# Forgetting attention and a GELU MLP on one core: batch 1's attention with its masks on TensorE and its side work reordered

## The chip, the cores and the metric

The kernel runs on one NeuronCore of a Trainium2 chip. The core has a matrix engine (TensorE, "PE" in the profile), a vector engine (VectorE, DVE), an activation engine (ScalarE, ACT), a general engine (GpSimd, POOL) and a queue engine (SyncE, SP) that starts transfers. The engines run side by side and wait for one another through semaphores. The metric is the device time of one execution in microseconds; lower is better.

## The reference, cut to what matters

Attention with a decay, over 8 batches of 8 heads, 576 tokens and 64 columns a head, then a two-layer MLP on the 4608 tokens:

```python
# q, k, v: (8, 8, 576, 64); f: (8, 8, 576); w_in: (512, 2048); w_out: (2048, 512)
scores = q @ k.T / sqrt(64)
cum    = cumsum(log(clip(f, 1e-4, 1)), axis=-1)
scores = where(causal, -1e9, scores + cum[..., :, None] - cum[..., None, :])
attn   = softmax(scores)
x      = (attn @ v), heads side by side          # (4608, 512)
h      = x @ w_in
out    = (0.5 * h * (1 + erf(h / sqrt(2)))) @ w_out
```

The kernel doesn't add the decay to the scores. The row's term cancels in the softmax, and the column's term becomes a weight exp(-cum) on the rows of v and on a column of ones beside them ("weighing"), whose product with the exponentials gives the softmax's sum. The causal mask only touches the five diagonal 128 x 128 blocks of a head; tokens 448 to 511 lie in two blocks and are weighted zero in one of them.

## The kernel before: the parts that the change touches

The program is one Python function whose order of calls is each engine's order of instructions. For each batch it does attention, head pair by head pair (HP = 4), with the second GEMM of the batch before as filling; then the first GEMM with GELU (`gemm1`). Batches 0 and 1 have attentions of their own. Pools give buffers in turn: two for scores (`s_psum`), two each of `o_psum` and `m_psum`, two for the tokens of q and of k (`qk_pool`), one for the weighed v (`v_pool`) and one for v itself.

One score tile: up to two products of kT and qT, the exponential, and the mask. `on_pe` chooses how the mask is made: on TensorE, as two more small products per diagonal block and head that add a large negative number to the future before the exponential, or on GpSimd, which sets the future to zero after it.

```python
def scores(b, i, t):
    on_pe = b == 0 or (b == 1 and i == 0)
    st = s_psum.tile([P, 2, 512], FP32, tag="s", name=f"s{t}")
    c = 0
    for n, q0, w in STILES[t]:
        masked = on_pe and c in SDIAG[t]
        for half in range(-1, 2 if masked else 0):
            for h in range(2):
                d = slice(h * D, (h + 1) * D)
                if half < 0:
                    to = st[:, h, c : c + w]
                    ab = kT[i][d, K0[n] : K0[n] + P], qT[i][d, q0 : q0 + w]
                else:
                    last = (half + 1) * D
                    to = st[:, h, c : c + last]
                    ab = key_of[d, half, :], after[d, half, 0:last]
                nc.tensor.matmul(to, *ab, start=half < 0, stop=half == 1 or not masked)
        c += w
    et = e_pool.tile([P, 2, 512], BF16, tag=f"e{t}", name=f"e{t}")
    nc.scalar.activation(et[:, :, 0:c], st[:, :, 0:c], Act.Exp, scale=scale)
    for c0 in [] if on_pe else SDIAG[t]:
        nc.gpsimd.affine_select(out=et[:, :, c0 : c0 + P], ...)   # cut
```

SDIAG has five entries over the four tiles of a head pair, so five masks a pair. The other pieces:

- `transposes_first(b, i, which, pool, tag)`: 12 TensorE transposes of the tokens of q (which 0) or k (1) of pair i into one buffer of the pool named, and a VectorE copy to qT or kT. Batches 0 and 1 are transposed so.
- `transpose_dma(b, h0, h1)`: the same by DMA for batches 2 and later, into `tq` and `tk`; `untangle(b, i)`: eight VectorE copies from there to qT and kT.
- `weigh_v(b, i)`: on GpSimd, the weighed v of a pair and its column of sums (two instructions). It needs v of the batch in place.
- `load_qk_tokens(b)`: GpSimd starts the loads of q and k of a batch. `load_v(b)`: SyncE starts five loads of v.
- `attend(b, i, h, ...)`: 15 products of exponentials and weighed v of one head ("AV"); `normalize`: a reciprocal and a multiplication on VectorE; `to_xT`: five TensorE transposes of a pair's result and a copy.

Batch 1's attention:

```python
FILL_1 = [[0, 0, 0, 0], [0, 0, 0, 0], [0, 0, 2, 2], [2, 2, 0, 0], [4]]

def second_attention():
    b, fill = 1, gemm2_half(0, 0)           # 16 products of batch 0's second GEMM

    def av(i, h):
        attend(b, i, h, (0, 1, 2, 3, 4))
        normalize(b, i, h)

    for i in range(HP):
        for t in range(4):
            scores(b, i, t)
            if (i, t) in ((0, 1), (0, 3)):
                for which in range(2):
                    transposes_first(b, 2 + t // 2, which, o_psum, "o")
            take(fill, FILL_1[i][t])
            if i and t == 1:
                av(i - 1, 0)
                av(i - 1, 1)
            if i and t == 3:
                to_xT(b, i - 1, nc.vector.tensor_copy, o_psum, "o")
            if (i, t) in ((1, 2), (2, 0)):
                weigh_v(1, i + 1)
            if (i, t) == (3, 0):
                load_qk_tokens(3)
                transpose_dma(2, 0, 4)
                transpose_dma(2, 4, 8)
    av(HP - 1, 0)
    take(fill, FILL_1[HP][0])
    av(HP - 1, 1)
    both = s_psum.tile([P, 2, 1024], BF16, tag="s", name="ps_x2")
    take(fill, 99)
    gemm1_begin(1, both)
    x_tail(1)
    load_v(2)
```

And the first GEMM's loop with what is threaded through it:

```python
for ffb in range(0 if b > 1 else 4, n_ff):      # n_ff = 16
    gemm1(b, ffb)
    if b == 0:
        if ffb in (13, 15):
            for which in range(2):
                transposes_first(1, ffb // 2 - 6, which, o_psum, "o")
        if ffb == 12:
            weigh_v(1, 0); load_w_out(0); load_w_out(1); weigh_v(1, 1)
            load_qk_tokens(2); load_w_out(2); load_w_out(3)
    elif b + 1 < B:
        first, gap = (5, 3) if b == 1 else (0, 4)
        at, late = divmod(ffb - first, gap)
        if late == 0:
            untangle(b + 1, at)
        if late == gap - 2:
            weigh_v(b + 1, at)
        if ffb == 14 and b > 1:
            load_qk_tokens(b + 2)
```

Although `load_qk_tokens(3)` is written ahead of `transpose_dma(2, ...)`, the built program makes GpSimd's loads of batch 3 wait for the semaphores of those DMA transposes.

Of the kernel before, what the change touches and what calls it, by code (L numbers as in the profile page):

```python
# [10 lines left out]
Act = mybir.ActivationFunctionType  # L11
# [7 lines left out]
HP = 4  # L19
# [31 lines left out]
def kernel(  # L51
# [10 lines left out]
    nc = tc.nc  # L62
# [24 lines left out]
    o_psum = ctx.enter_context(tc.tile_pool(name="o_psum", bufs=2, space=PSUM))  # L87
    m_psum = ctx.enter_context(tc.tile_pool(name="m_psum", bufs=2, space=PSUM))
# [4 lines left out]
    def load_qk_tokens(b, h0=0, h1=H):  # L93

        if b >= B:
            return
        if b not in qk_of:
            qk_of[b] = [
                qk_pool.tile([PT, H, JT * D], BF16, tag=n, name=f"{n}{b}")
                for n in "qk"  # L100
            ]
        for src, dst in zip((q, k), qk_of[b]):
            nc.gpsimd.dma_start(  # L103
                dst[:, h0:h1, :],
                src[b, h0:h1].rearrange("h (p j) d -> p h (j d)", j=JT),
            )
# [67 lines left out]
    warm = consts.tile([P, TC], BF16)  # L174
# [18 lines left out]
    def transposes_first(b, i, which, pool, tag):  # L193

        src = qk_of[b][which]
        ps = pool.tile([P, JT, PT], BF16, tag=tag, name="ps_f")
        for h in range(2):
            for j in range(JT):
                nc.tensor.transpose(
                    ps[h * D : (h + 1) * D, j, :],  # L200
                    src[:, 2 * i + h, j * D : (j + 1) * D],
                    ident_bf[:PT, :PT],
                )

        op = nc.scalar.copy if b == i == which == 0 else nc.vector.tensor_copy
        op(
            (qT, kT)[which][i].rearrange("d (p j) -> d p j", j=JT),
            ps.rearrange("d j p -> d p j"),
        )
# [3 lines left out]
    def transpose_dma(b, h0, h1):  # L213

        if b >= B:
            return
        if b not in tq_of:
            tq_of[b] = [
                tq_pool.tile([P, H, JT // 2, PT], BF16, tag="t" + n, name=f"t{n}{b}")
                for n in "qk"  # L220
            ]
        for src, dst in zip(qk_of[b], tq_of[b]):
            nc.sync.dma_start_transpose(  # L223
                dst[:, h0:h1].rearrange("d h j p -> d (h j) p"),
                src[:, h0:h1].rearrange("p h c -> p (h c)"),
            )
# [19 lines left out]
    def weigh_v(b, i, eng=nc.gpsimd):  # L246

        if b not in vw_of:
            vw_of[b] = v_pool.tile([P, H, NBLK, D + 1], BF16, tag="vw", name=f"vw{b}")
        hs = slice(2 * i, 2 * i + 2)  # L250
        bh = b * H + 2 * i
        w = wT[:, :, bh : bh + 2].rearrange("p n h -> p h n")
        eng.tensor_tensor(  # L253
            vw_of[b][:, hs, :, 0:D],
            v_sb[:, hs, :, :],
            w.unsqueeze(3).to_broadcast([P, 2, NBLK, D]),
            Alu.mult,
        )
        eng.tensor_copy(vw_of[b][:, hs, :, D], w)
# [1 line left out]
    e_of = {}  # L261

    def scores(b, i, t):
        on_pe = b == 0 or (b == 1 and i == 0)
        st = s_psum.tile([P, 2, 512], FP32, tag="s", name=f"s{t}")
        c = 0
        for n, q0, w in STILES[t]:
# [11 lines that stand above are left out]
                    nc.tensor.matmul(  # L279
                        to, *ab, start=half < 0, stop=half == 1 or not masked  # L280
                    )
            c += w
        et = e_pool.tile([P, 2, 512], BF16, tag=f"e{t}", name=f"e{t}")
        e_of[b, i, t] = et
        nc.scalar.activation(et[:, :, 0:c], st[:, :, 0:c], Act.Exp, scale=scale)  # L285
        for c0 in [] if on_pe else SDIAG[t]:
            nc.gpsimd.affine_select(  # L287
                out=et[:, :, c0 : c0 + P],
                in_=et[:, :, c0 : c0 + P],
                compare_op=Alu.is_ge,  # L290
                fill=0.0,
                base=0,
                pattern=[[0, 2], [1, P]],
                channel_multiplier=-1,
            )
# [3 lines left out]
    def attend(b, i, h, ms):  # L299
        if (b, i, h) not in o_of:  # L300
            o_of[b, i, h] = o_psum.tile([P, NBLK, D + 1], FP32, tag="o", name="o")
        o = o_of[b, i, h]
        for m in ms:
            for n in range(m + 1):
                t, c = where(n, m)
                nc.tensor.matmul(  # L306
                    o[:, m, :],
                    e_of[b, i, t][:, h, c : c + P],
                    vw_of[b][:, 2 * i + h, n, :],
                    start=(n == 0),  # L310
                    stop=(n == m),
                )
# [14 lines left out]
    def xT(b):  # L327
        if b not in xT_of:
            xT_of[b] = xT_pool.tile([P, n_dm, XC], BF16, tag="xT", name="xT")
        return xT_of[b]  # L330

    def to_xT(b, i, copy, pool=m_psum, tag="m", ps=None):
        if ps is None:
            ps = pool.tile([P, XC], BF16, tag=tag, name="ps_x")
        for m in range(NBLK):
            nc.tensor.transpose(
                ps[:, m * P : (m + 1) * P], x_of[b, i][:, m, :, :], ident_bf
            )
        copy(xT(b)[:, i, :], ps)  # L339
# [302 lines left out]
    def second_attention():  # L642


        b, fill = 1, gemm2_half(0, 0)

        def av(i, h):
            attend(b, i, h, (0, 1, 2, 3, 4))
            normalize(b, i, h)

        for i in range(HP):
            for t in range(4):
                scores(b, i, t)
                if (i, t) in ((0, 1), (0, 3)):
                    for which in range(2):
                        transposes_first(b, 2 + t // 2, which, o_psum, "o")
                take(fill, FILL_1[i][t])
                if i and t == 1:
                    av(i - 1, 0)
                    av(i - 1, 1)  # L660
                if i and t == 3:
                    to_xT(b, i - 1, nc.vector.tensor_copy, o_psum, "o")
                if (i, t) in ((1, 2), (2, 0)):
                    weigh_v(1, i + 1)
                if (i, t) == (3, 0):
                    load_qk_tokens(3)
                    transpose_dma(2, 0, 4)
                    transpose_dma(2, 4, 8)
        av(HP - 1, 0)
        take(fill, FILL_1[HP][0])  # L670
        av(HP - 1, 1)
# [6 lines that stand above are left out]
    for b in range(B):  # L678
        if b == 0:
            first_attention()  # L680
        elif b == 1:
            second_attention()
        else:
            attention(b)
        if b == 0:
            x_tail(0)
        for ffb in range(0 if b > 1 else 4, n_ff):
            gemm1(b, ffb)
            if b == 0:
                if ffb in (13, 15):  # L690
                    for which in range(2):
                        transposes_first(1, ffb // 2 - 6, which, o_psum, "o")
                if ffb == 12:
                    weigh_v(1, 0)
                    load_w_out(0)
                    load_w_out(1)
                    weigh_v(1, 1)
                    load_qk_tokens(2)
                    load_w_out(2)
                    load_w_out(3)  # L700
            elif b + 1 < B:
                first, gap = (5, 3) if b == 1 else (0, 4)
                at, late = divmod(ffb - first, gap)
                if late == 0:
# [5 lines that stand above are left out]
# [34 lines left out]
```

The softmax here doesn't subtract the row's maximum and nothing guards it: scores larger than these inputs give would overflow.

## Time and profile before

| | |
|---|---|
| device time, median of 3 (lowest to highest) | 363.75 us (363.01 to 365.11) |
| span of the profiled execution | 363.6 us |
| TensorE / ScalarE / VectorE / GpSimd busy | 94% / 59% / 53% / 35% |

The busy time of each engine by stretch of the profiled execution, read from its table of windows:

| stretch, us | what runs | TensorE | VectorE | ScalarE | GpSimd | TensorE clock |
|---|---|---|---|---|---|---|
| 0 to 24.5 | loads, attention 0 | 20.10 | 15.44 | 18.30 | 16.48 | 1.00 |
| 24.5 to 41.0 | first GEMM of batch 0 | 16.45 | 2.98 | 11.08 | 5.25 | 1.00 |
| 41.0 to 73.0 | attention 1 | 20.77 | 11.69 | 14.18 | 14.88 | 0.73 |
| 73.0 to 87.7 | first GEMM of batch 1 | 14.46 | 12.60 | 10.50 | 6.47 | 1.00 |
| 87.7 to 121.2 | attention 2, filled | 33.35 | 16.61 | 16.87 | 9.49 | 1.00 |
| 121.2 to 304.3 | batches 2 to 7 | 181.59 | 126.04 | 125.07 | 75.82 | 1.00 |
| 304.3 to 363.6 | last GEMMs | 55.69 | 7.38 | 19.10 | 0.40 | 0.99 |

How to read the profile's lines: "L287" is a line of the kernel; "out<-in" are the program's tiles; "x3" is the number of instructions merged into a line; a bracket at the end gives how long the engine had been idle before it and what ended that. In a timeline the first number is the start in us and the second the time that the line covers. A wait for several semaphores is put down to the one that came last by the profile. The clock is the share of full speed that TensorE was granted. The lines of this kernel that matter are: L279 score products and TensorE masks, L285 exponential, L287 GpSimd mask, L306 AV, L253 and L259 weighing, L103 token loads, L223 DMA transposes, L115 loads of v, L199 TensorE token transposes, L206 their copies, L237 untangling, L358 first GEMM, L484 and L449 second GEMM as filling.

### The profile page before, as it was taken

What the parts mean: (1) busy time and instruction counts of PE and PEld (TensorE: products, weight loads), DVE (VectorE), ACT (ScalarE), POOL (GpSimd) and SP (SyncE); (2) the same over time, 40 slices, a digit from 0 to 9 for tenths busy, and PEclk for the clock granted to TensorE, in tenths of its full rate; (3) what the DMA queues carried; (4) which work ended last, traced back from release to release, by engine and by line L of the source; (5) the groups of instructions that cost most, each with busy time, mean ns of one, the idle gap of its engine ahead of it and who ended that gap; (6) DMA issues with size and microseconds to landing.
All of it is one profiled execution on the core that took longest, in us unless ns stands there. A gap on an engine that the chain in (4) does not pass through costs nothing.

```text
span 363.6 us, 7947 instructions
## 1 busy us (share of the span) xinstructions
PE 342.4 (94%) x3232; PEld 179.9 (49%) x3232; DVE 192.7 (53%) x424; ACT 215.1 (59%) x295; POOL 128.8 (35%) x252
## 2 busy tenths in 40 slices
PE   7799886499999999999999999999999999999996
PEld 4574552244455445554555455545554555444443
DVE  5660442279346793579457955795579544011011
ACT  5977665077464378747874787478746874602610
POOL 8290762324332804452445344533451340000000
PEclk9999968599999999999999999999999999999999
DMA  8899999970978099919892899388920022011013
GB/s 126 153 176 192 192 196 191 184 120 2 196 144 162 29 138 211 160 59 130 166 199 69 124 149 205 87 120 160 203 80 2 32 65 77 0 57 60 0 31 87
DMA packets 99924, 43.03 MB, mean 118 GB/s; under 512 B 78704, under 2 KB 95344, under 8 KB 99888
## 3 DMA queue, kind: packets, MB, share of 16 engines
q1 hardware_dynamic: 82592, 28.37, 39.1%
q0 software_dynamic: 16896, 13.63, 25.1%
q8 instruction: 25, 0.41, 0.5%
q10 hardware_dynamic: 400, 0.52, 0.4%
q14 instruction: 11, 0.09, 0.1%
HBM read 36.85 MB, written 9.44 MB: 127 GB/s over the span
## 4 chain that ended last, share of the span: by engine, by line
PE 74%; DMA 10%; ACT 7%; POOL 5%; SPq 2%; issue 1%; DVE 0%; POOLq 0%; ACTq 0%; DVEq 0%
PE ps L358 30%; PE ps L449 20%; PE ps L391 8%; PE o L306 7%; PE s L279 5%; DMA k<-in_k_dram 5%; ACT e L285 4%; DMA v_sb<-in_v_dram 4%; PE ps L484 2%; ACT L285 2%; POOL vw L253 1%; DMA tq<-q 1%; POOL q L103 1%; SPq L223 1%; ACT g L375 1%
## 5 line engine op out<-in xcount | busy, mean ns | idle before, releaser
L375 ACT ACTIVATE g<-ps 128x512 bf16<-128x512 f32 x144 | 85.3, 597 | 79.3 <-PE ps L358 79.3
L285 ACT ACTIVATE e<-s 128x896 bf16<-128x896 f32 (+1 forms) x128 | 104.0, 863 | 35.2 <-PE s L279 34.2
L358 PE MATMUL ps<-xT,w_in_sb 128*128 128x512 bf16 x512 | 112.7, 379 | 0.2 <-ACT ot L493 0.2
L449 PE MATMUL ps<-w_out_sb,g 64*128 64x512 bf16 (+1 forms) x751 | 109.2, 376 | 0.0
L287 POOL TENSOR_SCALAR_AFFINE_SELECT e<-e 128x256 bf16<-128x256 bf16 x135 | 53.4, 406 | 111.3 <-ACT e L285 110.4
L358 PEld LDWEIGHTS <-w_in_sb 128*128 128x128 bf16 x576 | 56.0, 98 | 67.6 <-issue 2.3
L449 PEld LDWEIGHTS <-g 64*128 64x128 bf16 (+1 forms) x751 | 40.0, 94 | 30.8 <-issue 3.3
L237 DVE COPY qT<-tq 64x288 bf16<-64x288 bf16 x96 | 51.7, 539 | 1.4
L279 PE MATMUL s<-qT,kT 64*128 64x320 bf16 (+4 forms) x384 | 46.7, 285 | 5.5 <-ACT e L285 4.3
L306 PE MATMUL o<-vw,e 128*128 128x65 bf16 x960 | 42.4, 198 | 8.9 <-POOL e L287 8.6
L306 PEld LDWEIGHTS <-e 128*128 128x128 bf16 x960 | 37.4, 101 | 24.8 <-issue 10.0
L253 POOL TENSOR_TENSOR vw<-v_sb,wT 128x640 bf16<-128x640 f32 x31 | 39.7, 1281 | 15.6 <-DMA v_sb<-in_v_dram 11.2
L457 DVE COPY ot<-ps 128x512 f32<-128x512 f32 x26 | 17.9, 689 | 40.1 <-PE ps L449 40.1
L237 DVE COPY kT<-tk 64x288 bf16<-64x288 bf16 x96 | 33.8, 352 | 1.6
L279 PEld LDWEIGHTS <-kT 64*128 64x128 bf16 x384 | 20.2, 94 | 26.5 <-issue 14.2
L319 DVE RECIPROCAL r<-o 128x5 f32<-128x5 f32 x64 | 12.3, 192 | 39.0 <-PE o L306 38.5
L320 DVE TENSOR_TENSOR x<-o,r 128x320 bf16<-128x320 f32 x64 | 31.4, 491 | 2.4 <-DVE r L319 0.2
L400 DVE COPY ot<-ps 128x512 f32<-128x512 f32 (+2 forms) x9 | 5.7, 632 | 48.6 <-PE ps L391 48.6
L391 PE MATMUL ps<-w_out_sb,g 128*128 128x512 bf16 (+2 forms) x144 | 28.0, 355 | 0.0
L391 PEld LDWEIGHTS <-g 128*128 128x128 bf16 x144 | 13.5, 98 | 14.5
L459 DVE TENSOR_TENSOR ot<-ot,ps 128x512 f32<-128x512 f32 x26 | 17.9, 687 | 1.5
L348 POOL COPY tails<-xT 128x256 bf16<-128x256 bf16 x8 | 3.2, 399 | 34.4 <-DVE xT L339 34.4
(61 smaller groups left out, 162.1 us busy)
## 6 DMA issues: line engine op xcount, KB each, us to landing
out_dram<-ot SPq DMA_DIRECT2D x32, 256.0 KB, 2.2
v_sb<-in_v_dram SPq DMA_DIRECT2D x24, 256.0 KB, 4.6
q<-in_q_dram POOLq DMA_DIRECT2D x6, 576.0 KB, 6.0
k<-in_k_dram POOLq DMA_DIRECT2D x6, 576.0 KB, 8.6
v_sb<-in_v_dram SPq DMA_DIRECT2D x22, 128.0 KB, 5.8
w_in_sb<-in_moe_w_in_dram POOLq DMA_DIRECT2D x4, 512.0 KB, 7.4
w_out_sb<-in_moe_w_out_dram POOLq DMA_DIRECT2D x4, 512.0 KB, 12.0
q<-in_q_dram POOLq DMA_DIRECT2D x4, 144.0 KB, 4.0
```

Of the source, the lines that this page charges most:

```text
L237: nc.vector.tensor_copy(rows[:, odd], src[odd * D : (odd + 1) * D, 2 * i + h].rearrange("d j p -> d p j"),)
L253: eng.tensor_tensor(vw_of[b][:, hs, :, 0:D], v_sb[:, hs, :, :], w.unsqueeze(3).to_broadcast([P, 2, NBLK, D]), Alu.mult,)
L279: nc.tensor.matmul(to, *ab, start=half < 0, stop=half == 1 or not masked)
L285: nc.scalar.activation(et[:, :, 0:c], st[:, :, 0:c], Act.Exp, scale=scale)
L287: nc.gpsimd.affine_select(out=et[:, :, c0 : c0 + P], in_=et[:, :, c0 : c0 + P], compare_op=Alu.is_ge, fill=0.0, base=0, pattern=[[0, 2], [ ...
L306: nc.tensor.matmul(o[:, m, :], e_of[b, i, t][:, h, c : c + P], vw_of[b][:, 2 * i + h, n, :], start=(n == 0), stop=(n == m),)
L320: nc.vector.tensor_tensor(x_of[b, i][:, :, h, :], o[:, :, 0:D], r.unsqueeze(2).to_broadcast([P, NBLK, D]), Alu.mult,)
L358: nc.tensor.matmul(ps, w_in_sb[:, kt, ffb * P : (ffb + 1) * P], src[:, kt, 0:TC], start=(kt == 0), stop=(kt == n_dm - 1),)
L375: nc.scalar.activation(g_of[c][ffb], ps, Act.Gelu)
L391: nc.tensor.matmul(pss[ts][:, c0:c1], g_of[c][kt][:, ts * P : (ts + 1) * P], w_out_sb[:, kt, c0:c1], start=(kt == 0), stop=(kt == n_ff - 1),)
L449: nc.tensor.matmul(banks[r], g_of[c][kt][rows, ts * P : (ts + 1) * P], w_out_sb[rows, kt, :], start=(kt == 0), stop=last if r else kt == n ...
L457: nc.vector.tensor_copy(ot, banks[1])
```

## The change

Only batch 1 is changed, with what is threaded through the first GEMMs around it.

- All masks of batch 1 are made on TensorE, not only those of the first head pair. GpSimd has no mask left in that attention.
- The two heads' AV products, which stood together after tile 1 of the next pair, stand after tiles 1 and 2.
- The token transposes of pair 1 leave the first GEMM of batch 0; those of pairs 1, 2 and 3 follow the first three score tiles, in `o_psum`, `m_psum` and `o_psum`. Pair 0's come one block later than before (after block 14 instead of 13).
- `weigh_v` of pairs 2 and 3 is done ahead of the attention, as GpSimd's first work there.
- A 1 x 1 exponential ahead of the attention makes ScalarE load the exponential's table before the first scores are there.
- The transposes of a pair's result (`to_xT`) come one pair later, for the last two after the loop.
- `load_qk_tokens(3)` moves from the attention's last pair to block 4 of the first GEMM of batch 1, behind the attention and `x_tail`.

```diff
     def scores(b, i, t):
-        on_pe = b == 0 or (b == 1 and i == 0)
+        on_pe = b < 2
...
+        def transposes(i, pool, tag):
+            for which in range(2):
+                transposes_first(b, i, which, pool, tag)
+
+        nc.scalar.activation(warm[0:1, 0:1], warm[0:1, 0:1], Act.Exp)
+        weigh_v(1, 2)
+        weigh_v(1, 3)
         for i in range(HP):
             for t in range(4):
                 scores(b, i, t)
-                if (i, t) in ((0, 1), (0, 3)):
-                    for which in range(2):
-                        transposes_first(b, 2 + t // 2, which, o_psum, "o")
+                if i == 0 and t < 3:
+                    transposes(t + 1, *((m_psum, "m") if t == 1 else (o_psum, "o")))
                 take(fill, FILL_1[i][t])
-                if i and t == 1:
-                    av(i - 1, 0)
-                    av(i - 1, 1)
-                if i and t == 3:
-                    to_xT(b, i - 1, nc.vector.tensor_copy, o_psum, "o")
-                if (i, t) in ((1, 2), (2, 0)):
-                    weigh_v(1, i + 1)
+                if i and t in (1, 2):
+                    av(i - 1, t - 1)
+                if i > 1 and t == 0:
+                    to_xT(b, i - 2, nc.vector.tensor_copy, o_psum, "o")
                 if (i, t) == (3, 0):
-                    load_qk_tokens(3)
                     transpose_dma(2, 0, 4)
                     transpose_dma(2, 4, 8)
+        to_xT(b, HP - 2, nc.vector.tensor_copy, o_psum, "o")
         av(HP - 1, 0)
...
             if b == 0:
-                if ffb in (13, 15):
+                if ffb == 14:
                     for which in range(2):
-                        transposes_first(1, ffb // 2 - 6, which, o_psum, "o")
+                        transposes_first(1, 0, which, o_psum, "o")
...
             elif b + 1 < B:
+                if b == 1 and ffb == 4:
+                    load_qk_tokens(3)
                 first, gap = (5, 3) if b == 1 else (0, 4)
```

## The prediction

> **What bounds the kernel now.** I read the slices of the page first, then the chain of waits, then the timelines of single engines between 36 and 105 us, where the change lies. The page gives TensorE 94% busy, but its PE row has one hole and its PEclk row one dip, both between slices 5 and 8 (9.09 us each, so 45 to 73 us): batch 1's attention. Everything after 75 us is paced by TensorE without gaps, so a change in this stage is worth what it moves the start of that gapless part. The chain of waits there:
>
> ```profile
> 43.46 12.26 DMA k<-in_k_dram
> 55.73 3.97 SPq L223
> 59.76 4.79 DMA tq<-q
> ...
> 65.14 0.84 POOL q L103
> ...
> 66.62 0.77 POOL k L103
> 67.40 0.78 POOL e L287 x2
> ```
>
> From 43 to 68 us no arithmetic is on the chain. The tokens of batch 2 land, are transposed by DMA, only then may GpSimd issue the load of batch 3, and only then does it come to three masks of batch 1's last head pair. TensorE's own timeline shows the price:
>
> ```profile
> 60.43 0.22 PE L306 MATMUL o<-vw,e 128*128 128x65 bf16 x2
> 68.23 1.08 PE L306 MATMUL o<-vw,e 128*128 128x65 bf16 x13 [7.57 <-POOL e L287]
> 69.12 1.90 PE L484 MATMUL ps<-w_out_sb,g 128*128 128x512 bf16 x4
> ...
> 72.97 0.59 PE L358 MATMUL ps<-xT,w_in_sb 128*128 128x512 bf16 x2
> ...
> 87.66 0.37 PE L279 MATMUL s<-qT,kT 64*128 64x256 bf16 x4
> ```
>
> 7.57 us idle, then four projection matmuls in 1.90 us, about twice what eight take later. The first GEMM of batch 1 starts at 72.97 and attention 2 at 87.66, so that stage is 14.69 us. GpSimd over the same time:
>
> ```profile
> 57.94 0.77 POOL L287 TENSOR_SCALAR_AFFINE_SELECT e<-e 128x256 bf16<-128x256 bf16 x2 [0.92 <-ACT e L285]
> 65.14 0.84 POOL L103 DMA_DIRECT2D q<-in_q_dram  x1 [6.44 <-DMA tq<-q]
> 66.62 0.77 POOL L103 DMA_DIRECT2D k<-in_k_dram  x1 [0.64 <-DMA tk<-k]
> 67.40 1.12 POOL L287 TENSOR_SCALAR_AFFINE_SELECT e<-e 128x256 bf16<-128x256 bf16 x3
> ...
> 80.05 1.40 POOL L253 TENSOR_TENSOR vw<-v_sb,wT 128x640 bf16<-128x640 f32 x1 [4.37 <-PE ps L358]
> ```
>
> The last line is the one I come back to: weighing for batch 2 starts at 80.05. TensorE, which the view names, had long been done with batch 1's values; asking for batch 2's v load by its tile shows who it was. Its last transfer is issued at 67.9 and needs 12.0 us, which is 79.9:
>
> ```profile
> L115 SPq DMA_DIRECT2D v_sb<-in_v_dram x1: 5374/5374/5374, 67.9 to 67.9; - x1
> ...
> DMA to landing us min/median/max: 12.0/12.0/12.0
> ```
>
> Last, what a stage of this kind costs when masks are on TensorE: batch 0's attention, by ScalarE and TensorE.
>
> ```profile
> 14.94 7.40 ACT L285 ACTIVATE e<-s 128x640 bf16<-128x640 f32 x9 [0.56 <-PE s L279]
> ...
> 19.27 0.37 PE L279 MATMUL s<-qT,kT 64*128 64x320 bf16 x4
> 19.47 0.25 PE L279 MATMUL s<-after,key_of 64*128 64x64 bf16 x4
> 19.66 0.65 PE L306 MATMUL o<-vw,e 128*128 128x65 bf16 x15
> 20.24 0.36 PE L279 MATMUL s<-qT,kT 64*128 64x448 bf16 x2
> ```
>
> Nine exponentials in 7.40 us, 0.82 each; a masked score tile 0.39 (19.27 to 19.66), one head's AV product 0.58 (19.66 to 20.24).
>
> [...]three selects whose inputs were ready by about 61 us run at 67.40, behind two loads.[...]after the transposes at 41.8 to 45.0 with gaps of 1.03 and 0.36 us, the granted clock of this trace was 0.50 at 46 to 48 us; but batch 0, with transposes too, kept 1.00.[...]the rows of the table loads have a mean of 1283 ns.
>
> **The change part by part.** I date the new stage from rows of this trace, at full clock.
>
> 1. Start. One pair of token transposes (q and k of a head pair, 0.75 to 1.1 us) now lies ahead of the last gelu block instead of two. The scores begin about 40.3 instead of 41.0, when VectorE has copied kT. The gelu that ends at about 41.0 is followed by the table load without waiting for scores: 41.0 + 1.28 + about 0.15 for the 1x1 exponential (my estimate) puts the first real exponential at 42.4 instead of 42.93. Worth 0.5 us at most.
>
> 2. Masks. 15 selects of 0.39 us leave GpSimd; 15 mask groups of four matmuls join TensorE, about 0.09 to 0.14 us each by batch 0's starts, 1.8 us in all. They are real TensorE time, but the AV products no longer wait for GpSimd: its two waits of 1.00 and 7.57 us go.
>
> 3. Loads and weighing. The load of batch 3 now stands after the attention, so it blocks no mask. Two weighings of 1.46 us (1.27 + 0.19) move to the front: the second half of v lands at 36.9 + 6.6 = 43.5, GpSimd is free at 45.8, so both are done by 48.8, and the first AV product to need them comes at about 54.
>
> 4. TensorE's sum. Score tiles by batch 0's starts: 0.47, 0.39, 0.38, 0.32 = 1.56 us for a head pair. Pair 0: 1.56 + 3 transposes x 1.10 = 4.9. Pair 1: 1.56 + 2 AV x 0.58 = 2.7, but ScalarE needs 3 x 0.82 + 0.65 = 3.1, so 3.1. Pairs 2 and 3: 2.7 + 0.29 (x transposes, 21.52 to 21.81) + 4 fills x 0.216 = 3.9 each. Tail: 0.29 + 2 x 0.58 + 8 x 0.216 = 3.2, and about 0.5 waiting for the last exponential. Sum 4.9 + 3.1 + 3.9 + 3.9 + 3.7 = 19.5. From 40.3: the GEMM starts at 59.8, against 72.97. The clock may fall to half for one window, as it did here at 46 us[...]. So 61.3 rather than 59.8, and attention 2 starts at 61.3 + 14.7 = 76.0, 11.7 us sooner.
>
> 5. What does not move. Batch 2's tokens land at 52.9 and 55.7 and its DMA transposes end at 64.6 and 66.0 whatever TensorE does, since nothing ahead of them in their queues changes. Hence the load of batch 3 still goes out near 65 to 67, load_v(2) still follows the transposes at 64.0, and v still lands near 80. VectorE's untangling of batch 2 (32 copies, about 11 us at 0.335) can start at 62.6 and is done by 74, just ahead of attention 2: hidden. GpSimd weighs four times from 80.05 to 86.1 and then, in order, comes to batch 2's first five selects, 5 x 0.39, up to 88.1. Before, attention 2's first AV pair ended at 100.70 (13.04 after its start). Now it cannot end before 88.1 plus about 0.7 for the matmuls behind the last select, 88.8. By step 4 it would end at 76.0 + 13.0 = 89.0. The two limits nearly meet, so I expect 89.0, a gain of 11.7 us. Even without a cold window (GEMM at 59.8, pair done at 87.5) the select would take back 1.3 us, leaving 11.9.
>
> After that each stage is TensorE's and keeps its length; batch 3's transposes and loads stand in queues that were free in time and move with it. 363.75 - 11.7 = 352.0 us.
>
> **The rivals.** (a) A cold clock throughout. The new stage is a string of small matmuls waiting on ScalarE; if half clock held from 43 to 60, TensorE would pay some 6 us more, attention 2 would start at 80, and the gain would be 7 to 8: 356. For it: 0.50 to 0.65 at 45 to 49 and 52 to 55 here, each after gaps of about 1 us. Against: batch 0's like stage ran at 1.00, with TensorE 3 of 4 us busy. (b) A new wait on v of batch 2, as in step 5, larger than I think: were v to land at 83[...], the gain would be near 9, so 355. Against it: the same transfers start at the same times. (c) The hidden wait is not the load but the transposes: were untangling not to be done at 74, scores would wait. 0.335 us per copy while GpSimd is idle speaks against it; the slow ones here (four in 4.69 us from 81.67) lie exactly under the weighing, which is now elsewhere. (d) Masks on TensorE merely lengthen the bound engine: 1.8 us added and no wait removed would give 365. The 7.57 us wait in the trace speaks against it.
>
> **Range and chances.** Both limits of step 5 give 88.8 to 89.0, which makes the middle stiff: 352. Downward there is little, only v landing a little sooner and no cold window: 350.2. Upward a second cold window or a late v: 355.5. Faster by over 2% means under 356.5, for which 0.93; within 2% 0.06; slower 0.01.
>
> **What would show it.** TensorE's timeline should have no idle piece over 1 us from 40 to 61 us and GEMM 1's first matmul at 60 to 62 (step 4); ScalarE's table load right behind the last gelu (step 1); GpSimd's token loads still near 65 and weighing at 80, then selects back to back from 86 (step 5); a TensorE wait for a GpSimd select of up to 1.3 us at the first AV pair of attention 2. It would be wrong if the DMA transposes or v land elsewhere, or if the clock column stays at 0.5 for more than one window between 43 and 60 us.

## The result, and the profile after

| | before | changed |
|---|---|---|
| device time, median (lowest to highest), us | 364.0 (363.01 to 365.11) | 353.18 (352.45 to 353.55) |
| executions | 4 | 4 |
| span of the traced execution, us | 363.6 | 350.1 |

The changed kernel takes 0.9699 of the time before, with a 95% interval of 0.9666 to 0.9733: about 10.8 us less, where 11.7 were predicted. The two traced spans differ by 13.5 us. That overstates the gain: the traced execution of before took 365.64 us, above its median, and that of the changed kernel 352.91, below its own, and of these times 2.0 and 2.8 us lie outside the spans. So the gain is read from the medians, and the traces only show where it came from.

The page of the changed kernel, TensorE's busy share and its granted clock in 40 slices:

```profile
PE   7799998999999999999999999999999999999995
...
PEclk9999999999999999999999999999999999999999
```

The hole and the dip between slices 5 and 8 are gone. TensorE's timeline of the changed kernel, with the marks that the prediction dated, and after it the first AV pair of attention 2 in the trace before:

```profile
39.97 0.28 PE L279 MATMUL s<-qT,kT 64*128 64x256 bf16 x2 [0.29 <-DVE kT L206]
...
45.44 0.87 PE L306 MATMUL o<-vw,e 128*128 128x65 bf16 x15
...
56.35 0.45 PE L336 MATMUL ps_x<-ident_bf,x 128*128 128x128 bf16 x5 [0.49 <-DVE x L320]
56.64 0.64 PE L306 MATMUL o<-vw,e 128*128 128x65 bf16 x15
...
59.32 0.59 PE L358 MATMUL ps<-xT,w_in_sb 128*128 128x512 bf16 x2
...
74.01 0.36 PE L279 MATMUL s<-qT,kT 64*128 64x256 bf16 x4
...
86.00 1.11 PE L306 MATMUL o<-vw,e 128*128 128x65 bf16 x30
```

```profile
99.65 1.11 PE L306 MATMUL o<-vw,e 128*128 128x65 bf16 x30
```

Attention 1 runs from 39.97 to 59.32 with no idle piece over 0.5 us. The first GEMM starts 13.65 us sooner than in the trace before (72.97), attention 2 as much (74.01 against 87.66), and its first AV pair too (86.00 against 99.65): what was gained in attention 1 is kept. GpSimd's timeline of the changed kernel:

```profile
46.16 1.28 POOL L253 TENSOR_TENSOR vw<-v_sb,wT 128x640 bf16<-128x640 f32 x1
...
61.62 0.40 POOL L348 COPY tails<-xT 128x256 bf16<-128x256 bf16 x1 [14.02 <-DVE xT L339]
64.55 0.84 POOL L103 DMA_DIRECT2D q<-in_q_dram  x1 [2.53 <-DMA tq<-q]
65.97 0.93 POOL L103 DMA_DIRECT2D k<-in_k_dram  x1 [0.59 <-issue]
78.55 1.28 POOL L253 TENSOR_TENSOR vw<-v_sb,wT 128x640 bf16<-128x640 f32 x1 [11.65 <-DMA v_sb<-in_v_dram]
...
84.06 2.92 POOL L287 TENSOR_SCALAR_AFFINE_SELECT e<-e 128x256 bf16<-128x256 bf16 x8
```

The first token load still waits for a DMA transpose, and the two go out at 64.55 and 65.97 (65.14 and 66.62 before). The weighing for batch 2 starts at 78.55 (80.05 before), and this time the view names the v load itself, after 11.65 us of idling. The selects follow it without a gap. Eight take 2.92 us, so the five of pair 0 end at about 84.06 + 5 x 0.365 = 85.9, and the AV pair that needs them starts at 86.00 without a wait. That looks like no slack at all; four of the experiments put it at 0.6 to 0.9 us. ScalarE at the start of attention 1:

```profile
39.71 0.60 ACT L375 ACTIVATE g<-ps 128x512 bf16<-128x512 f32 x1 [1.12 <-PE ps L358]
40.33 1.28 ACT L656 ACT_TABLE_LOAD   x1
41.62 0.21 ACT L656 ACTIVATE warm<-warm 1x1 bf16<-1x1 bf16 x1
41.73 4.90 ACT L285 ACTIVATE e<-s 128x896 bf16<-128x896 f32 x6
```

The table load stands directly behind the last gelu, and six exponentials follow without a gap.

### The profile page after: what moved, and what is told of

Read it like the earlier page. It is cut to its first block, busy times and chain, and to the rows that moved or that the text cites. A ratio compares the mean times of both kernels' runs of the same rounds, so it can differ in the third digit from the quotient of the medians.

```text
span 350.1 us, 8011 instructions
## 1 busy us (share of the span) xinstructions
PE 335.7 (96%) x3250; PEld 179.0 (51%) x3292; DVE 188.7 (54%) x424; ACT 215.6 (62%) x296; POOL 122.8 (35%) x237
## 3 DMA queue, kind: packets, MB, share of 16 engines
q1 hardware_dynamic: 82592, 28.37, 40.4%
## 4 chain that ended last, share of the span: by engine, by line
PE 83%; ACT 9%; issue 2%; POOL 2%; DMA 2%; DVE 1%; ACTq 0%; POOLq 0%; DVEq 0%
PE ps L358 35%; PE ps L449 20%; PE o L306 9%; PE ps L391 8%; PE s L279 7%; ACT e L285 5%; PE ps L484 2%; ACT L285 2%; DMA k<-in_k_dram 2%; ACT g L375 1%; PE ps_x L336 1%; POOL q L103 1%; DVE x L320 1%; POOL k L103 1%; PE ps_f L199 0%
## 5 line engine op out<-in xcount | busy, mean ns | idle before, releaser
L449 PE MATMUL ps<-w_out_sb,g 64*128 64x512 bf16 (+1 forms) x726 | 103.3, 376 | 1.6 <-issue 0.8
L287 POOL TENSOR_SCALAR_AFFINE_SELECT e<-e 128x256 bf16<-128x256 bf16 x120 | 47.6, 408 | 94.2 <-ACT e L285 93.4
L237 DVE COPY qT<-tq 64x288 bf16<-64x288 bf16 x96 | 48.5, 506 | 1.7 <-DMA tq<-q 0.3
L306 PEld LDWEIGHTS <-e 128*128 128x128 bf16 x960 | 35.7, 98 | 15.7 <-issue 9.1
L306 PE MATMUL o<-vw,e 128*128 128x65 bf16 x960 | 40.7, 194 | 0.7
L391 PEld LDWEIGHTS <-g 128*128 128x128 bf16 x144 | 13.5, 98 | 14.5
L348 POOL COPY tails<-xT 128x256 bf16<-128x256 bf16 x8 | 3.2, 398 | 41.8 <-DVE xT L339 41.8
```

Source lines behind the costliest of these rows:

```text
L237: nc.vector.tensor_copy(rows[:, odd], src[odd * D : (odd + 1) * D, 2 * i + h].rearrange("d j p -> d p j"),)
L287: nc.gpsimd.affine_select(out=et[:, :, c0 : c0 + P], in_=et[:, :, c0 : c0 + P], compare_op=Alu.is_ge, fill=0.0, base=0, pattern=[[0, 2], [ ...
L306: nc.tensor.matmul(o[:, m, :], e_of[b, i, t][:, h, c : c + P], vw_of[b][:, 2 * i + h, n, :], start=(n == 0), stop=(n == m),)
L391: nc.tensor.matmul(pss[ts][:, c0:c1], g_of[c][kt][:, ts * P : (ts + 1) * P], w_out_sb[:, kt, c0:c1], start=(kt == 0), stop=(kt == n_ff - 1),)
L449: nc.tensor.matmul(banks[r], g_of[c][kt][rows, ts * P : (ts + 1) * P], w_out_sb[rows, kt, :], start=(kt == 0), stop=last if r else kt == n ...
```

## The experiments

All ratios are to the kernel before, run on the same chip in the same round (medians there 364.66 to 364.82 us).

| kernel | median us (range) | ratio, 95% interval |
|---|---|---|
| the load moved, alone | 356.77 (356.19 to 357.88) | 0.9781 [0.9736, 0.9827] |
| masks on TensorE, alone | 354.64 (354.23 to 355.94) | 0.9725 [0.968, 0.9771] |
| both of these | 354.35 (353.26 to 354.53) | 0.9702 [0.9649, 0.9754] |
| changed, masks back on GpSimd | 352.81 (352.22 to 353.66) | 0.9671 [0.9627, 0.9715] |
| changed, load back | 353.19 (352.73 to 353.43) | 0.9681 [0.9638, 0.9724] |
| changed, masks and load back | 364.19 (363.05 to 366.41) | 0.9989 [0.9969, 1.0009] |
| changed, no early table | 353.48 (352.42 to 354.73) | 0.9689 [0.9656, 0.9722] |
| changed, two more weighings | 358.05 (354.59 to 359.58) | 0.9801 [0.9748, 0.9854] |
| changed, four more weighings | 359.73 (358.01 to 361.82) | 0.9866 [0.9825, 0.9906] |
| changed, again | 353.14 (352.32 to 355.12) | 0.9695 [0.9665, 0.9724] |
| changed, load after weighing | 352.84 (352.75 to 354.79) | 0.9685 [0.9657, 0.9713] |
| changed, load after weighing, masks back on GpSimd | 352.59 (351.61 to 354.91) | 0.9684 [0.965, 0.9717] |

**The load moved, alone.** The kernel before, with

```diff
                 if (i, t) == (3, 0):
-                    load_qk_tokens(3)
                     transpose_dma(2, 0, 4)
...
             elif b + 1 < B:
+                if b == 1 and ffb == 4:
+                    load_qk_tokens(3)
```

> The kernel before with one thing changed: the load of batch 3's tokens stands in the first GEMM of batch 1, not in attention 1. Theory (the 7.57 us wait of TensorE is GpSimd's load standing ahead of three masks; whatever parts the two removes it): the last AV product waits for the masks about 0.6 us instead of 7.57, the 4.7 us of matmuls behind it run at full clock and not at half, so the first GEMM starts near 64 instead of 73 and the time is about 355 (354 to 356.5). Rival (masks on TensorE are what helps, the load is only where the wait shows): 361 or more.

356.77 us: 8 us of gain from one line moved, 0.3 above the range given. TensorE's timeline of this kernel:

```profile
52.06 1.56 PE L306 MATMUL o<-vw,e 128*128 128x65 bf16 x25 [1.00 <-POOL e L287]
...
60.74 0.27 PE L306 MATMUL o<-vw,e 128*128 128x65 bf16 x3 [0.37 <-POOL e L287]
61.34 0.49 PE L306 MATMUL o<-vw,e 128*128 128x65 bf16 x10 [0.33 <-POOL e L287]
...
63.86 0.59 PE L358 MATMUL ps<-xT,w_in_sb 128*128 128x512 bf16 x2
```

Instead of 7.57 us the last AV product waits 0.37 + 0.33, and the GEMM starts at 63.86, where 64 was expected. The wait of 1.00 us for a mask behind a weighing is still there, and the clock was 0.58 from 52 to 56 us behind it.

**Masks on TensorE, alone.** The kernel before, with

```diff
-        on_pe = b == 0 or (b == 1 and i == 0)
+        on_pe = b < 2
```

> The kernel before with one thing changed: all masks of batch 1 on TensorE, the load of batch 3 left inside attention 1. Theory: GpSimd still stands at the load until about 65, but nothing of attention 1 is behind it, so the same wait goes: about 355 (353.5 to 356.5), and the other wait of 1.00 us goes too. Rival (the parts add up, each worth about half): 358 to 360.

354.64 us. GpSimd still stood at the load, longer than ever; its timeline and then TensorE's in this kernel:

```profile
66.10 0.84 POOL L103 DMA_DIRECT2D q<-in_q_dram  x1 [16.79 <-DMA tq<-q]
```

```profile
57.64 0.49 PE L306 MATMUL o<-vw,e 128*128 128x65 bf16 x10 [0.33 <-ACT e L285]
...
60.17 0.59 PE L358 MATMUL ps<-xT,w_in_sb 128*128 128x512 bf16 x2
...
87.88 1.33 PE L306 MATMUL o<-vw,e 128*128 128x65 bf16 x28 [0.81 <-POOL e L287]
```

16.79 us of waiting on GpSimd cost TensorE nothing, because nothing of attention 1 stood behind it. The last line is the second limit of the prediction's step 5, seen at work: v landed late in this execution (the weighing began at 80.83, against 78.55 in the changed kernel), and the first AV pair of attention 2 waited 0.81 us for a select.

**Both.** The two edits above together.

> The kernel before with both: masks of batch 1 on TensorE and the load moved. Theory: both remove the same wait, so together they give no more than the masks alone, within 0.7 us: about 354.5; what is left to the changed kernel (about 1.3 us) comes from the spread transposes, the split AV products and the weighing ahead. Rival (parts add up): equal to the changed kernel, 353.2, and well below either part alone.

354.35 us, against 354.64 for the masks alone. The parts are worth 8.1 and 10.2 us alone and 10.5 together: they don't add up, because both take away the same wait. What is left to the changed kernel is 1.2 us (354.35 to 353.14, on another chip). The intervals of the two ratios overlap, so this remainder isn't shown to be more than noise.

**The changed kernel with the masks back on GpSimd.**

```diff
-        on_pe = b < 2
+        on_pe = b == 0 or (b == 1 and i == 0)
```

> The changed kernel with the masks of batch 1's pairs 1 to 3 back on GpSimd; all else as changed. Theory: the masks are made a whole pair ahead of their AV products, so only the last pair waits, about 0.4 us; TensorE saves 15 mask groups, up to 1.8 us, of which ScalarE's exponentials let about 1 through. But attention 2's first AV pair then comes to within GpSimd's selects (pair 0 done at 86.0), which takes it back: 353.2 within 0.7.[...] Rival (masks on TensorE are the gain): 360 or more.

352.81 us, not to be told from the changed kernel. TensorE in this kernel:

```profile
40.61 0.28 PE L279 MATMUL s<-qT,kT 64*128 64x256 bf16 x2 [0.29 <-DVE kT L206]
...
56.73 0.49 PE L306 MATMUL o<-vw,e 128*128 128x65 bf16 x10 [0.15 <-POOL e L287]
...
59.26 0.59 PE L358 MATMUL ps<-xT,w_in_sb 128*128 128x512 bf16 x2
...
86.50 1.33 PE L306 MATMUL o<-vw,e 128*128 128x65 bf16 x28 [0.34 <-POOL e L287]
```

The last pair's mask costs 0.15 us, not 0.4. From the first scores to the GEMM this kernel needs 59.26 - 40.61 = 18.65 us, the changed one 59.32 - 39.97 = 19.35: the 15 mask groups cost TensorE 0.7 us of the path in these two traces, not 1.8. In five other traces of the new order with masks on TensorE the stretch is 19.45 to 20.34 us, so the cost varies from 0.7 to 1.7 us. Attention 2 gives 0.34 of it back here: v landed later than in the changed kernel's trace (weighing from 79.45 instead of 78.55). So the headline of the change, masks on TensorE, is one of two ways to remove the wait, and with the load moved and the rest reordered it isn't needed. In the old order it still helps beside the moved load: 354.35 us with both against 356.77, on the same chip and with ranges that don't overlap.

**The load back, masks on TensorE.** The changed kernel with `load_qk_tokens(3)` at (3, 0) again.

> The changed kernel with only the load of batch 3 back inside attention 1, masks on TensorE. Theory: GpSimd stands at the load until about 65, but has nothing else to do for attention 1; equal to the changed kernel within 0.8 us (352.4 to 354). Rival (the place of the load matters by itself): 356 or more.

353.19 us against 353.14: either of the two is enough.

**Neither.** The changed kernel with both edits undone, so that only the reordering is left.

> The changed kernel with the masks of pairs 1 to 3 back on GpSimd and the load of batch 3 back inside attention 1: only the reordering is left (early table, spread transposes, weighing ahead, split AV products). Theory: the last three masks again stand behind a load that cannot go out before the DMA transposes end, near 65, and those do not move; TensorE resumes near 68.5 at half clock whatever was saved ahead of it. So the reordering alone gives nothing: 363 to 365, with a TensorE wait for GpSimd of 9 to 11 us, longer than the 7.57 of before. Rival (the reordering is worth its 1 to 2 us by itself): 361.5 to 362.5.

364.19 us, ratio 0.9989 with 1 inside the interval, over 20 executions. TensorE, and then GpSimd, in this kernel:

```profile
68.22 1.08 PE L306 MATMUL o<-vw,e 128*128 128x65 bf16 x13 [9.11 <-POOL e L287]
```

```profile
65.17 0.83 POOL L103 DMA_DIRECT2D q<-in_q_dram  x1 [8.55 <-DMA tq<-q]
66.61 0.77 POOL L103 DMA_DIRECT2D k<-in_k_dram  x1 [0.61 <-DMA tk<-k]
67.39 1.12 POOL L287 TENSOR_SCALAR_AFFINE_SELECT e<-e 128x256 bf16<-128x256 bf16 x3
```

TensorE resumes at 68.22, where before it was 68.23. The reordering brought it to the wait sooner, although attention 1 began later in this execution (43.07 instead of 41.01), and the wait grew from 7.57 to 9.11 us. A saving ahead of a wait for transfers was worth nothing here while the wait stood.

Then it counts. With the load moved, the same reordering takes 4.0 us off (356.77 to 352.81, on one chip, with intervals that don't overlap); with the masks on TensorE it takes 1.5 us off (354.64 to 353.19), which isn't clear of the spread. Part of this may be the clock: of the four traces with the old order that of the kernel before shows it at 0.50 from 46 to 48 us, and those of the load moved alone and of both edits show means of 0.64 and 0.66 from 44 to 48 us; with the masks alone it was 1.00 there, and so it was in the new order in the changed kernel and in the one with its masks back on GpSimd. Which part of the reordering does that was not tested.

**No early table.** The changed kernel without the 1 x 1 exponential.

> The changed kernel without the 1 x 1 exponential. In its trace the last gelu ends at 40.31 and the first scores at about 40.5, so without it the table load would start at 40.5 instead of 40.33, and the 1 x 1 exponential's 0.21 us go. Theory by the trace: no difference, within 0.4 us. Rival, my prediction's step 1: 0.5 us slower.

353.48 us against 353.14, within the spread of either. ScalarE in this kernel:

```profile
39.85 0.60 ACT L375 ACTIVATE g<-ps 128x512 bf16<-128x512 f32 x1 [1.11 <-PE ps L358]
40.73 1.28 ACT L285 ACT_TABLE_LOAD   x1 [0.28 <-PE s L279]
42.03 3.29 ACT L285 ACTIVATE e<-s 128x896 bf16<-128x896 f32 x4
```

The load waits 0.28 us for the scores; with the early exponential it waits nothing, but that instruction takes its own 0.1 to 0.2 us. Because the scores now come so soon, the trick buys nothing that can be measured.

**Two, and then four more weighings.** The changed kernel, with the last weighing of batch 2 repeated on GpSimd (same values written again):

```diff
                 if late == gap - 2:
-                    weigh_v(b + 1, at)
+                    for _ in range(3 if (b, at) == (1, 3) else 1):    # then 5
+                        weigh_v(b + 1, at)
```

> The changed kernel with two more weighings of batch 2's last pair on GpSimd (the same values written again), 2 x 1.38 = 2.8 us between the landing of v and attention 2's first masks. In the changed kernel's trace pair 0's five selects end near 85.9 and its AV product starts at 86.0: no slack. Theory: TensorE waits 2.5 to 3 us there and the time grows by as much, to 355.5 to 356.3. Rival (GpSimd has slack there and the next stages take it up): 353.2, as the changed kernel.

358.05 us: 4.9 us more, where 2.5 to 3 were expected. The traced execution was the lowest of the four, 354.59 us. Its selects and its first AV pair of attention 2:

```profile
86.71 2.92 POOL L287 TENSOR_SCALAR_AFFINE_SELECT e<-e 128x256 bf16<-128x256 bf16 x8
```

```profile
87.16 0.23 PE L306 MATMUL o<-vw,e 128*128 128x65 bf16 x2 [0.16 <-POOL e L287]
88.24 1.33 PE L306 MATMUL o<-vw,e 128*128 128x65 bf16 x28 [0.84 <-POOL e L287]
```

The selects began 2.65 us later than in the changed kernel's trace (84.06), attention 2 began 0.84 us later (74.85 instead of 74.01), and TensorE waited 1.00 us. So the changed kernel had about 0.8 us of slack there (2.65 - 0.84 - 1.00, an estimate). This trace doesn't explain the median. The other three executions had a mean clock of 0.995 instead of 0.998, and in them v may also have landed later: the start of the weighing lies between 77.75 and 80.83 us in the traces whose token load stands ahead of it. The clock suggested a dose that makes a longer wait:

> The changed kernel with four more weighings on GpSimd, 4 x 1.38 = 5.5 us. Two more cost 4.9 us by the median (358.05), though the one traced execution lost only 1.4; the untraced ones had a mean clock of 0.995 and not 0.998. Theory: the wait grows by the weighings[...]: 359.5 to 361.5, with the clock at 0.5 behind the wait in the trace. Rival (each weighing costs more than its 1.38 in this place): 363 or more.

359.73 us, within the range. TensorE and GpSimd's selects with four more weighings, and the table of windows over the wait (columns: stretch, its length, busy time of TensorE, weight loads, VectorE, ScalarE and GpSimd, then the granted clock, the share of DMA and GB/s):

```profile
91.93 0.29 PE L306 MATMUL o<-vw,e 128*128 128x65 bf16 x2 [4.91 <-POOL e L287]
93.01 1.91 PE L306 MATMUL o<-vw,e 128*128 128x65 bf16 x28 [0.79 <-POOL e L287]
```

```profile
91.48 2.92 POOL L287 TENSOR_SCALAR_AFFINE_SELECT e<-e 128x256 bf16<-128x256 bf16 x8
```

```profile
88.00:90.00 2.00, 0.00 (x0) 0.00 (x0) 0.01 (x1) 0.00 (x0) 2.00 (x4) 1.00 0.00 0
90.00:92.00 2.00, 0.07 (x2) 0.07 (x2) 0.00 (x0) 0.00 (x0) 2.00 (x5) 0.51 0.00 0
92.00:94.00 2.00, 1.20 (x17) 0.87 (x18) 0.00 (x0) 0.00 (x0) 2.00 (x6) 0.50 0.75 172
94.00:96.00 2.00, 2.00 (x23) 1.21 (x22) 1.37 (x4) 0.48 (x1) 0.40 (x2) 0.50 1.32 234
96.00:98.00 2.00, 2.00 (x18) 0.89 (x16) 0.00 (x0) 1.14 (x2) 0.41 (x1) 0.78 1.36 228
```

The wait is 4.91 + 0.79 = 5.70 us. It isn't the 5.5 us of added work alone, since v landed later too: the selects began 7.42 us after those of the changed kernel, and attention 2 only 0.86 us later (74.87). That leaves about 0.9 us of slack (7.42 - 0.86 - 5.70); the same sum gives 0.6 for the waits of 0.81 and 0.34 us above, whose selects began at 86.34 and 84.97 and whose attention 2 at 74.85 and 73.95. So the chain has less than 1 us of slack, and all beyond it is waited for. Behind the wait the clock is 0.50: 28 AV matmuls take 1.91 us instead of the 1.11 that 30 take in the changed kernel. That two weighings cost 4.9 us by the same route in the untraced executions fits their clock, but no trace shows it, and a later v would fit as well; it stays open.

**The load after the weighing.** The changed kernel with

```diff
-                if b == 1 and ffb == 4:
+                if b == 1 and ffb == 14:
                     load_qk_tokens(3)
```

> The changed kernel with the load of batch 3's tokens after GpSimd's third weighing instead of ahead of the first. Theory: v of batch 2 no longer shares the transfers with 1.2 MB of tokens and lands well before 79, near 72; the weighing and attention 2's masks follow, so that the second limit (masks ready at 86 for an AV product at 86) is gone. TensorE's own work is the other limit and stays, so the time falls by the waits that some executions show there, 0 to 0.8 us: 352.5 to 353.2. Rival (weighing is bound by TensorE's progress, as the view of waits names it): no shift of the weighing at all.

352.84 us. GpSimd in this kernel:

```profile
72.51 1.28 POOL L253 TENSOR_TENSOR vw<-v_sb,wT 128x640 bf16<-128x640 f32 x1 [9.66 <-DMA v_sb<-in_v_dram]
...
76.79 0.84 POOL L103 DMA_DIRECT2D q<-in_q_dram  x1
77.62 0.78 POOL L103 DMA_DIRECT2D k<-in_k_dram  x1
```

The weighing starts at 72.51 instead of 78.55. The five loads of v go out at the same times in both traces (63.4 or 63.5 to 66.9 or 67.0), but the slowest takes 6.2 instead of 12.0 us to land: v lands six microseconds sooner when the two token loads go out at 76.79 and 77.62 and not, at 64.55 and 65.97, among its own. The landing of v was the limit, not TensorE. The time moves by 0.3 us, which isn't clear of the spread: the first AV pair of attention 2 starts at 86.80 here, without a wait, right behind TensorE's own work.

**Load late and masks on GpSimd.** The last edit and the masks' together.

> The load placed late, and also the masks of batch 1's pairs 1 to 3 back on GpSimd. Theory: with those masks on GpSimd the stretch from the first scores of batch 1 to its first GEMM was 18.65 us against 19.35, and what attention 2 gave back there (a wait of 0.34) is gone with the late load: 0.7 us under the changed kernel, 352.0 to 352.8. Rival (the tail of the last pair's masks and the clock take it back): equal to the late load alone or slower.

352.59 us (351.61 to 354.91), the lowest median of all, but its interval [0.965, 0.9717] covers the changed kernel's 0.9695. The traced span was 349.7, and no wait of TensorE for GpSimd at attention 2 was left. A version that clearly beats the changed kernel was not found.

## Why the prediction was right, point by point

- **What bounded it** (a chain of transfers ending at three masks behind two loads): shown. Taking the load from ahead of the masks, or the masks from behind the load, takes the wait away; undoing both brings it back to the full time.
- **Step 1, start:** the scores began at 39.97 (40.3 predicted), the first exponential at 41.73 (42.4; the table load took 1.28 us and the 1 x 1 exponential 0.21, for which 0.15 was a guess that rested on no row), which is 1.2 us sooner than in the trace before and not 0.5. But this start differs between executions: 40.36 to 41.01 in the four traces of the old order, 39.78 to 40.61 in eight of the new one and 43.07 in a ninth. What the step is worth was not measured, and the table load has no measurable share in it.
- **Step 2, masks:** both waits for GpSimd went. The 1.8 us that the mask groups were to cost are 0.7 on the path of this trace, up to 1.7 in others. That ScalarE's exponentials cover the rest is an assumption that was not shown.
- **Step 3, weighing:** the second weighing's product ended at 47.44 (all done by 48.8 predicted); no AV product waited for it.
- **Step 4, the sum:** 19.5 us by rows of batch 0, 19.35 measured from the first scores to the GEMM. What was mis-sized is the clock term: I added 1.5 us for a stretch at half clock, an estimate. The trace before shows two such stretches: 0.64, 0.50, 0.50 and 0.65 in the four microseconds from 45 to 49, and 0.55, 0.50, 0.50 and 0.74 in those from 52 to 56; summed, 1.7 us are lost in each. In the traced execution of the changed kernel the clock stayed at 1.00 from 38 to 64 us. Of six executions in the repeat, two had a mean of 0.993 and 0.994 and took 355.12 and 354.80 us, the others 0.998 to 1.000 and 352.32 to 353.29. So such a stretch may come in some executions, though no trace of the changed kernel shows one, and the term may have been right as a chance rather than as a cost. One reading behind it is put wrongly: the four projection matmuls of 1.90 us did not take "about twice what eight take later" but the same 1.90 us as eight (at 87.95), which is twice as long for each.
- **Step 5, what does not move:** loads at 64.55, weighing at 78.55, pair 0's masks ready at about 85.9, the AV pair at 86.00. The predicted 80, 88.1 and 89.0 for the pair's end came 1.5 to 2.2 us sooner (the end was 87.1), for two separate reasons: v landed sooner in this execution, and the first GEMM began at 59.32 instead of 61.3. Both limits moved by about the same, which is luck; so they still "nearly meet", with 0.6 to 0.9 us between them. That was the sharpest point of the prediction, and it held: v later by 2.3 and 0.9 us shows as 0.81 and 0.34 us of waiting in two of the kernels above. The wait of up to 1.3 us that was named as a sign did not come.
- **The sum:** 11.7 us predicted, 10.8 by the medians, and that these lie so close is partly luck. From trace to trace the first AV pair of attention 2 came 13.65 us sooner (99.65 to 86.00), 2 us more than predicted, because no stretch at half clock came and v landed sooner. Against that, I measured the old stage on an execution of 365.64 us and took the gain off a median of 363.75, 1.9 us lower. The two errors nearly cancel.
- **Rivals:** (a), a clock at half throughout, and (d), masks that only lengthen TensorE's work, are refuted by the trace. (b), a limit by v, is real but small here, and large (up to 6.6 us, half clock included) once something is added to GpSimd's chain. (c): untangling took 1.34 to 1.57 us for four copies and ended at 73.2, before attention 2's first scores at 74.01: hidden.

## What to carry to other kernels

An engine that both starts transfers and does small work for another engine can pass the transfer's wait on to that engine. Here GpSimd came to three masks only at 67.40 us, behind two loads, though the exponentials that they mask had ended at 61.08, and TensorE waited 7.57 us. Look at what stands behind a load in such an engine's queue, and move either one, since moving both pays only once (8.1 and 10.2 us alone, 10.5 together). A saving ahead of a wait for a transfer was worth nothing here until that wait was gone (a ratio of 0.9989 for the reordering alone, 4.0 us once the load was moved); then ask at once which transfer sets the next limit, and test its slack by adding work to that chain. A wait of TensorE can be paid twice, as the wait and as matmuls at half clock behind it: the clock was 0.50 from 68 to 72 us after the wait of 7.57 us, 0.60 on average from 68 to 74 us after that of 9.11, 0.50 from 92 to 96 us with that of 4.91, and after one of 1.00 us it was 0.50 to 0.55 from 52 to 55 us in one trace and 0.58 on average from 52 to 56 in another. After one of 0.84 us it was 1.00.

## What the runs showed of the hardware that was not expected

- In three of the kernels (two and four more weighings; the load after the weighing) TensorE stood for 0.65, 0.91 and 1.05 us behind the twelfth matmul of batch 1's first AV product, for nothing that the trace shows. In the changed kernel those 15 matmuls took 0.87 us instead of 0.65. Six traces of the new order with masks on TensorE show it (0.79 to 1.87 us from the start of the first to the end of the fifteenth), the three with masks on GpSimd don't (0.65 us). It moves the first GEMM by up to 1 us from one execution to the next; its cause is open.
- In the changed kernel 72 token transposes of 0.21 us lie between 40.4 and 43.9 us, with one gap of 0.30 us among them, and the clock stayed at 1.00. In the trace before 48 of them lie between 41.8 and 46.2 us, with gaps of 1.03 and 0.36 us, and the clock was 0.50 from 46 to 48 us. But the kernel with masks on TensorE alone had the same two gaps, and its clock was 1.00 from 40 to 78 us. So neither the transposes nor these gaps alone account for the lower clock; its cause is open.
- In the wait of 4.91 us, from 87.02 to 91.93, the clock was 1.00 from 88 to 90 us and 0.51 from 90 to 92. It was still 0.50 from 92 to 96 and 0.78 on average from 96 to 98 us, with a second wait of 0.79 us before 93.01, and 1.00 from 98 to 100.
